# A gated attention, a dense and a routed expert layer in one kernel: routing steps with stated waits, own tiles for one expert's second weights, one ring of four PSUM banks, 512-token dense layers 2 and 3

## Chip, cores and metric

One core of a Trainium2 chip. The metric is the device time of one execution in microseconds, the median of three runs. One execution is also profiled; its rows are read below.

## What is computed

```python
def _attn_ref(q, k, v, alpha):                     # 2 x 8 heads, 768 steps, 48 wide
    for t in range(S):
        state = alpha[:, :, t, :, None] * state + np.einsum('bhd,bhe->bhde', k[:, :, t], v[:, :, t])
        y[:, :, t] = np.einsum('bhd,bhde->bhe', q[:, :, t], state)

def _moe_ref(x, domain_probs, w1, w2):             # 1536 tokens x 384, 4 experts, 1024 hidden
    p = domain_probs / (domain_probs.sum(-1, keepdims=True) + 1e-09)
    for e in range(E):
        out += p[:, e:e + 1] * (np.maximum(x @ w1[e], 0.0) @ w2[e])

def _moe2_ref(x, w_gate, w_noise, noise, w1, w2):  # 8 experts, the best two of each token
    noisy = x @ w_gate + np.log1p(np.exp(x @ w_noise)) * noise
    top2 = np.argpartition(-noisy, 2, axis=1)[:, :2]
    top2_w = softmax of the two noisy logits
    out[token] += top2_w[token, k] * (np.maximum(x[token] @ w1[e], 0.0) @ w2[e])
```

The attention's output, with the heads side by side, is the x of the dense layer, whose output is the x of the routed one.

## The kernel before

Everything is one program on one core, its order written out by hand: generators emit instructions step by step, and each engine works through its own in that order. The work goes through these stages.

The attention runs in groups of 128-token blocks, woven into dense expert 0. Dense experts 1 and 2 (`for e in range(1, E1 - 1)`, line 952) run alone, in units of 384 tokens. Dense expert 3 runs in `main` (line 970), with the routing of the layer behind it as the `side` generator (line 958). Then come eight routed experts on gathered rows, in falling order of their load. The fullest is taken as expert `E1` + 0 (called expert 4 here, the next expert 5), whatever its number.

A matrix product in full precision is made of three: each operand is split into a high half (rounded to fp32r) and the rest, and low x high, high x low and high x high are added up in PSUM. `Weights` loads a quarter of one weight matrix at a time into one of four `raw` tiles (on SP's DMA queue), ACT copies out the high half (line 137), and GpSimd (to expert 4) or DVE (after it) subtracts for the low half (line 138). `W.step`, called at each main step, emits one such preparation as soon as the tiles that it overwrites have been used (`self.done`).

One unit of an expert is 8 calls of `hidden` (line 446; 9 matmuls into one PSUM bank, `hh` by ACT at line 461, `hl` by DVE at line 462, which frees the bank) and then, per block of 128 tokens, 24 matmuls of `product` (line 466) into one bank, read by DVE into `acc` (line 499). Each call of `hidden`, and each 6 matmuls of `product`, is a main step. `hidden` takes its banks from a ring of two (`g1`), `product` from another ring of two (`g2`). Two more banks are `tr`, one each `sc0` and `sc1`.

`drive` (line 506) runs main steps and lets 1.3 steps of `side` follow each. A bare `yield` in `side` is one such step. `route(g)` takes three 128-token blocks: when their rows are done, TensorE turns them (`turned_rows`), makes the gate's logits, and `choose` (line 623) goes on: `uu`, `sp` by ACT; `dl`, `nl`, the maxima and their indices, `sel` and `mask` by DVE; rank matmuls (lines 666 to 672); `spos`, `pos`, `row`, `ge`, `Aoh`, `wt`, `B4`, `VB`, `BV` by DVE; 12 matmuls (line 716) that add these rows to the lists of each expert in `sc0`. After three of four groups, `all_but_last` makes the row numbers `ig_a` of the first two slots of expert 4, gathers their rows (`xg`, an indirect DMA issued on GpSimd), and `side` turns them (`turn`, line 857; `xth` by ACT, `xtl` by DVE). Expert 4 starts on these 256 rows (`moe2(0, 0, 2)`) while the last group is routed. `the_last` then does the same with `ig_b` for the other two slots, ranks the experts by load (`places`), starts the loads of expert 5's weights, whose number SP reads from `places`, and makes the lists of all others (`ig_c`). The other two slots are turned, and `moe2` goes on.

## Time and profile before

| what | us |
|---|---|
| median of 3 runs | 787.21 |
| lowest of 3 runs | 786.96 |
| the profiled execution, its own time | 787.36 |
| its span, first to last instruction | 785.6 |
| TensorE busy in it | 760.1 |
| DVE busy | 351.6 |
| ACT busy | 250.1 |
| GpSimd busy | 170.1 |

The span is what the rows speak of; 1.76 us of the profiled execution lie around it. The ends of matmuls are modelled and overlap the next one's start, so the cost of a matmul is read from start to start, and a busy share of TensorE near 100% doesn't say that it computes at its peak.

### The profile page before, as it was taken

What the parts mean: (1) busy time and instruction counts of PE and PEld (TensorE: products, weight loads), DVE (VectorE), ACT (ScalarE), POOL (GpSimd) and SP (SyncE); (2) the same over time, 40 slices, a digit from 0 to 9 for tenths busy, and PEclk for the clock granted to TensorE, in tenths of its full rate; (3) what the DMA queues carried; (4) which work ended last, traced back from release to release, by engine and by line L of the source; (5) the groups of instructions that cost most, each with busy time, mean ns of one, the idle gap of its engine ahead of it and who ended that gap; (6) DMA issues with size and microseconds to landing.
All of it is one profiled execution on the core that took longest, in us unless ns stands there. A gap on an engine that the chain in (4) does not pass through costs nothing.

```text
span 785.6 us, 12222 instructions
## 1 busy us (share of the span) xinstructions
PE 760.1 (97%) x4774; PEld 734.3 (93%) x4774; DVE 351.6 (45%) x856; ACT 250.1 (32%) x497; POOL 170.1 (22%) x177
## 2 busy tenths in 40 slices
PE   7999999999999999999999999989899999999994
PEld 5889999999999999999999999988799999999994
DVE  5677665763222222222222425445664554554540
ACT  2433222232411223111122313424344444444330
POOL 2410000000510013100041000143342424423331
PEclk7799999999999999999999999999999999999998
DMA  9844412100630003100032000120664655655510
GB/s 169 188 112 88 85 31 41 22 1 1 191 91 1 1 20 101 41 1 1 20 89 67 18 31 10 58 85 11 215 190 131 195 165 153 193 179 164 161 61 30
DMA packets 97998, 66.97 MB, mean 85 GB/s; under 512 B 57577, under 2 KB 94500, under 8 KB 97936
## 3 DMA queue, kind: packets, MB, share of 16 engines
q1 hardware_dynamic: 89008, 51.92, 25.0%
q0 software_dynamic: 5024, 14.13, 5.7%
q8 instruction: 39, 0.64, 0.4%
q10 hardware_dynamic: 3904, 0.10, 0.4%
q14 instruction: 23, 0.19, 0.1%
HBM read 56.69 MB, written 9.82 MB: 85 GB/s over the span
## 4 chain that ended last, share of the span: by engine, by line
PE 68%; issue 14%; POOL 7%; DVE 4%; DMA 4%; ACT 1%; POOLq 0%; DVEq 0%; ACTq 0%
PE g L470 9%; PE g L472 9%; PE g L471 9%; PE g L456 9%; PE g L457 9%; PE g L458 9%; POOL pv L853 2%; PE tr L279 2%; PE sc L371 2%; POOL xg L853 2%; DMA out_dram<-yo,si_c 2%; PE sc L331 2%; POOL out_dram L883 2%; PE sc L345 1%; PE sc L367 1%
## 5 line engine op out<-in xcount | busy, mean ns | idle before, releaser
L461 ACT ACTIVATE hh<-g 128x384 fp32r<-128x384 f32 (+7 forms) x216 | 99.4, 461 | 288.1 <-PE g L458 283.6
L462 DVE SCALAR_TENSOR_TENSOR hl<-g,hh 128x384 fp32r<-128x384 f32 (+7 forms) x216 | 112.3, 521 | 168.6 <-ACT hh L461 168.4
L470 PE MATMUL g<-w2h,hl 128*128 128x384 f32 x464 | 161.0, 347 | 0.0
L472 PE MATMUL g<-w2h,hh 128*128 128x384 f32 x464 | 156.9, 338 | 0.0
L471 PE MATMUL g<-w2l,hh 128*128 128x384 f32 x464 | 156.7, 338 | 0.0
L456 PE MATMUL g<-xh,w1l 128*128 128x384 f32 (+1 forms) x408 | 134.9, 331 | 1.0 <-DVE hl L462 1.0
L457 PE MATMUL g<-xl,w1h 128*128 128x384 f32 (+1 forms) x408 | 131.7, 323 | 0.0
L458 PE MATMUL g<-xh,w1h 128*128 128x384 f32 (+1 forms) x408 | 131.5, 322 | 0.0
L138 POOL TENSOR_TENSOR w1l<-raw,w1h 128x768 fp32r<-128x768 f32 x20 | 37.4, 1876 | 323.2 <-ACT w1h L137 191.3
L471 PEld LDWEIGHTS g<-w2l,hh 128*128 128x128 f32 x464 | 87.5, 189 | 0.0
L470 PEld LDWEIGHTS g<-w2h,hl 128*128 128x128 f32 x464 | 87.3, 188 | 0.2
L472 PEld LDWEIGHTS g<-w2h,hh 128*128 128x128 f32 x464 | 87.2, 188 | 0.0
L456 PEld LDWEIGHTS g<-xh,w1l 128*128 128x128 f32 x408 | 76.7, 188 | 2.2 <-DVE hl L462 2.2
L457 PEld LDWEIGHTS g<-xl,w1h 128*128 128x128 f32 x408 | 76.8, 188 | 0.3 <-DVE xl L396 0.3
L458 PEld LDWEIGHTS g<-xh,w1h 128*128 128x128 f32 x408 | 76.7, 188 | 0.0
L456 PE MATMUL g<-xth,w1l 128*128 128x256 f32 (+6 forms) x216 | 73.9, 342 | 2.6 <-DVE hl L462 1.5
L499 DVE SCALAR_TENSOR_TENSOR acc<-g,prob,acc 128x384 f32<-128x384 f32 x36 | 22.2, 617 | 118.8 <-PE g L472 118.8
L457 PE MATMUL g<-xtl,w1h 128*128 128x256 f32 (+6 forms) x216 | 71.3, 330 | 0.2 <-DVE xtl L868 0.2
L458 PE MATMUL g<-xth,w1h 128*128 128x256 f32 (+6 forms) x216 | 71.3, 330 | 0.0
L137 ACT ACTIVATE w2h<-raw 128x768 fp32r<-128x768 f32 x44 | 37.2, 845 | 29.1 <-issue 16.1
L883 POOL DMA_INDIRECT out_dram<-yo,si_c x26 | 27.0, 1039 | 86.9 <-DVE yo L882 83.8
L456 PEld LDWEIGHTS g<-xth,w1l 128*128 128x128 f32 x216 | 40.7, 188 | 4.0 <-issue 1.6
(182 smaller groups left out, 1070.6 us busy)
## 6 DMA issues: line engine op xcount, KB each, us to landing
raw<-in_moe_w_dram SPq DMA_DIRECT2D x92, 384.0 KB, 3.3
v<-in_v_dram SPq DMA_DIRECT2D x12, 192.0 KB, 3.8
out_dram<-zero SPq DMA_DIRECT2D x1, 2304.0 KB, 11.1
x2d<-acc SPq DMA_DIRECT2D x12, 192.0 KB, 1.9
x_a<-in_alpha_dram SPq DMA_DIRECT2D x20, 96.0 KB, 3.0
x_k<-in_k_dram SPq DMA_DIRECT2D x18, 96.0 KB, 3.1
x_q<-in_q_dram SPq DMA_DIRECT2D x18, 96.0 KB, 3.2
acc<-in_moe_w_dram SPq DMA_DIRECT2D x4, 384.0 KB, 5.6
```

The lines of the kernel that those rows point to most:

```text
L137: nc.scalar.activation(hi, r, AF.Copy)
L138: (nc.gpsimd if e <= E1 else nc.vector).tensor_sub(lo, r, hi.bitcast(F32))
L456: nc.tensor.matmul(t[:, :n], wl, hx[:, kd, t0:t0 + n], start=(kd == 0), stop=False)
L457: nc.tensor.matmul(t[:, :n], wh, lx[:, kd, t0:t0 + n], start=False, stop=False)
L458: nc.tensor.matmul(t[:, :n], wh, hx[:, kd, t0:t0 + n], start=False, stop=(kd == KD - 1))
L461: nc.scalar.activation(hh[:, :n], t[:, :n], AF.Relu)
L462: nc.vector.scalar_tensor_tensor(hl[:, :n], t[:, :n], 0.0, hh.bitcast(F32)[:, :n], op0=OP.max, op1=OP.subtract)
L470: nc.tensor.matmul(t[:m, :DM], hl[:, o:o + m], wh, start=(f == 0), stop=False)
L471: nc.tensor.matmul(t[:m, :DM], hh[:, o:o + m], wl, start=False, stop=False)
L472: nc.tensor.matmul(t[:m, :DM], hh[:, o:o + m], wh, start=False, stop=(f == KF - 1))
L853: nc.gpsimd.indirect_dma_start(out=t[:n, :], out_offset=None, in_=out if prev else x2d[:upto, :], in_offset=bass.IndirectOffsetOnAxis(ap=S ...
L883: nc.gpsimd.indirect_dma_start(out=parts_of_out[s], out_offset=bass.IndirectOffsetOnAxis(ap=SLOT[e * SB + s][2][:n, e * SB + s:e * SB + s ...
```

## The change

The order of preparation takes expert 4's second weights before its first, into a pool of their own (`ownpool`, open from dense expert 3 on), subtracted on GpSimd; its first weights are subtracted on DVE. Expert 5's second weights wait for dense expert 3's only. All first- and second-layer outputs share one ring of four banks (`g`; where `ps("g2", 2)` stood, `ps("g", 4)` stands). Dense experts 1 and 2 take units of 512 tokens, their hidden tiles in a pool `hpool`, whose place `ownpool` takes after them. In `drive`, what `side` yields is the number of main steps until its next step. `choose` works in bursts with stated waits. The first gathered slots are turned in step with the last group's routing (`together`). The loads of expert 5's weights are emitted after the gather of its rows, and SP reads from a copy of `places`.

```diff
@@ Weights
-            self.order = [(e, t, g) for e in range(E1 + E2) for t in ((1, 2) if e else (2, 1))
+            self.order = [(e, t, g) for e in range(E1 + E2) for t in ((2, 1) if e in (0, E1) else (1, 2))
                           for g in range(NG)]
...
-            hi = wpool.tile([P, KD * FG * P], F32R, tag=f"w{t}h", name=f"w{t}h", bufs=NG)
-            lo = wpool.tile([P, KD * FG * P], F32R, tag=f"w{t}l", name=f"w{t}l", bufs=NG)
+            own = (e, t) == (E1, 2)
+            pool = self.own if own else wpool
+            hi = pool.tile([P, KD * FG * P], F32R, tag=f"w{t}h", name=f"w{t}h", bufs=NG)
+            lo = pool.tile([P, KD * FG * P], F32R, tag=f"w{t}l", name=f"w{t}l", bufs=NG)
             nc.scalar.activation(hi, r, AF.Copy)
-            (nc.gpsimd if e <= E1 else nc.vector).tensor_sub(lo, r, hi.bitcast(F32))
+            (nc.gpsimd if e < E1 or own else nc.vector).tensor_sub(lo, r, hi.bitcast(F32))
...
-                if e == 0 or (e - 1, t, g) in self.done:
+                if (e, t) == (E1, 2):
+                    free = self.own is not None
+                elif t == 2 and e == E1 + 1:
+                    free = (e - 2, t, g) in self.done
+                else:
+                    free = e == 0 or (e - 1, t, g) in self.done
+                if free:
                     self.prep()
@@ hidden
+    hidden_in = [(wpool, CAP)]
     def hidden(e, f, hx, lx, t0, n, H_):
-        t = ps("g1", 2)
+        t = ps("g", 4)
...
-        hh = wpool.tile([P, CAP], F32R, tag=f"hh{f}", name="hh")
-        hl = wpool.tile([P, CAP], F32R, tag=f"hl{f}", name="hl")
+        pool, cap = hidden_in[-1]
+        hh = pool.tile([P, cap], F32R, tag=f"hh{f}", name="hh")
+        hl = pool.tile([P, cap], F32R, tag=f"hl{f}", name="hl")
@@ drive
         due = 0.0
+        pace = n_main / n_side if n_side else float("inf")
+        wait = pace
...
-            due += n_side / n_main
-            while side is not None and due >= 1:
-                due -= 1
+            due += 1
+            while side is not None and due >= wait:
+                due -= wait
                 try:
-                    next(side)
+                    said = next(side)
+                    wait = pace if said is None else said
@@ before dense expert 1
+    hst = ExitStack()
+    hidden_in.append((hst.enter_context(tc.tile_pool(name="hpool", bufs=1, side="right")), 4 * P))
@@ choose
         V_.tensor_mul(dl, dl, w)
-        yield
+        yield 2
...
         V_.tensor_add(nl, tl[:, :, :E2], nl)
-        yield
...
             V_.max_index(mi[:, i, :], mx[:, i, :], nl[:, i, :])
-        yield
...
         nc.scalar.activation(ex, ex, AF.Exp)
-        yield
-        yield
+        yield 2
...
         nc.tensor.matmul(o, ones_b, sofar[:, None, :].to_broadcast(b3), start=False, stop=True)
-        yield
...
             V_.tensor_reduce(pos, spos.rearrange("x c b e -> x (c b) e"), axis=AX.X, op=OP.add)
-        yield
...
                          row[:, :, None].to_broadcast([P, 2 * UB, P]), op=OP.is_equal)
+        yield 1
...
         V_.tensor_mul(wt[:, 1, :], ex, wt[:, 0, :])
-        yield
-        if not last:
-            yield
...
                              VB[:, j, :, None, :].to_broadcast(b5), op=OP.mult)
-        yield
-        yield
-        yield
-        yield
+        yield 3
@@ route
+        for i in range(BL):
             while b0 + i not in rows_done:
-                yield
-            yield
...
+                yield 0.5
+            yield 1
+            turned_rows(g, i, b0 + i)
+            yield 1
+            logits(g, i)
         yield from choose(g, b0, BL)
@@ the_last
-        W.ranked = places
-        while W.n_raw - W.n_prep < 4:
-            W.load()
...
         gather(1, 0, blocks(1))
+        nc.vector.tensor_copy(ordered, places)
+        W.ranked = ordered
+        while W.n_raw - W.n_prep < 4:
+            W.load()
@@ dense experts 1 and 2, and side
-        for t0 in range(0, N, 3 * P):
-            drive(moe1(e, t0, 3 * P), bg=W.step)
+        for t0 in range(0, N, 4 * P):
+            drive(moe1(e, t0, 4 * P), bg=W.step)
+    hidden_in.pop()
+    hst.close()
+    own = ExitStack()
+    W.own = own.enter_context(tc.tile_pool(name="ownpool", bufs=1, side="right"))
...
+    def together(*gens):
+        now = 0.0
+        due = [(0.0, i, g) for i, g in enumerate(gens)]
+        while due:
+            due.sort(key=lambda z: z[:2])
+            t, i, g = due.pop(0)
+            if t > now:
+                yield t - now
+                now = t
+            said = next(g, "done")
+            if said != "done":
+                due.append((now + said, i, g))
...
         yield from all_but_last()
-        yield
-        for i in range(2):
-            yield
-            turn(0, i)
-        turned.append(True)
-        yield from route(NB // BL - 1)
+        def first_rows():
+            for i in range(2):
+                yield 6 - 4 * i
+                turn(0, i)
+            turned.append(True)
+        yield from together(first_rows(), route(NB // BL - 1))
         yield from the_last()
```

## Rows read from the trace of the kernel before

**Rows 1.** The page's first part: busy us (share of the span) x instructions.
```profile
PE 760.1 (97%) x4774; PEld 734.3 (93%) x4774; DVE 351.6 (45%) x856; ACT 250.1 (32%) x497; POOL 170.1 (22%) x177
```

**Rows 2.** Stretches: us, then busy us (x instructions) by engine, granted clock, DMA share, GB/s.
```profile
core 0: us, PE busy (x) PEld busy (x) DVE busy (x) ACT busy (x) POOL busy (x), PEclk, DMA share, GB/s
...
200.00:500.00 300.00, 300.00 (x1760) 298.97 (x1759) 82.24 (x193) 71.22 (x133) 43.36 (x47) 1.00 0.15 45
500.00:560.00 60.00, 51.81 (x345) 48.54 (x344) 33.62 (x118) 21.56 (x42) 26.67 (x24) 1.00 0.27 84
560.00:774.00 214.00, 213.33 (x1240) 208.12 (x1239) 113.61 (x172) 93.22 (x160) 76.83 (x75) 1.00 0.50 155
```

**Rows 3.** Waits of TensorE: who waited for whom, us in total, times, longest.
```profile
PE g L456 <- DVE hl L462: 2.5, 4, 1.0
PE tr L865 <- DMA xg<-x2d,ig_b: 1.8, 1, 1.8
PE sc L716 <- DVE BV L706: 1.5, 1, 1.5
PE tr L865 <- DMA xg<-x2d,ig_a: 1.4, 1, 1.4
...
PE g L456 <- ACT xth L867: 0.6, 1, 0.6
...
PE g L456 <- DVE sp L643: 0.5, 1, 0.5
```

**Rows 4.** Timeline of TensorE: start us, us, instruction (384, 256 and 432 columns).
```profile
258.25 0.34 PE L456 MATMUL g<-xh,w1l 128*128 128x384 f32 x1
...
270.74 0.34 PE L470 MATMUL g<-w2h,hl 128*128 128x384 f32 x1
...
531.11 0.28 PE L456 MATMUL g<-xth,w1l 128*128 128x256 f32 x1
...
532.76 0.29 PE L458 MATMUL g<-xth,w1h 128*128 128x256 f32 x1
...
576.75 0.36 PE L456 MATMUL g<-xth,w1l 128*128 128x432 f32 x1
...
590.50 0.36 PE L458 MATMUL g<-xth,w1h 128*128 128x432 f32 x1
```

**Rows 5.** Timeline of DVE in the hand-over: groups 2 and 3 of the choice.
```profile
506.46 1.72 DVE L659 TENSOR_TENSOR mask<-sel 128x24 bf16<-128x24 f32 x1
...
537.35 0.17 DVE L643 TENSOR_TENSOR sp<-sp,dl 128x24 f32<-128x24 f32 x1
...
539.73 0.18 DVE L659 TENSOR_TENSOR mask<-sel 128x24 bf16<-128x24 f32 x1
...
543.20 0.19 DVE L675 TENSOR_TENSOR spos<-sel,tr 128x48 f32<-128x48 f32 x1
...
543.87 0.96 DVE L686 TENSOR_TENSOR Aoh<-iota_i,row 128x768 f32<-128x768 int32 x1
...
546.01 0.63 DVE L706 TENSOR_TENSOR BV<-sel,VB 128x192 f32<-128x192 f32 x2
...
553.13 0.19 DVE L736 SCALAR_TENSOR_TENSOR si_c<-LR,emp 128x32 int32<-128x32 f32 x1
```

**Rows 6.** Groups of DVE by shape: count, busy us, mean ns, idle before and releaser.
```profile
L462 DVE SCALAR_TENSOR_TENSOR hl<-g,hh 128x384 fp32r<-128x384 f32 x120 | 66.7, 556 | 116.7 <-ACT hh L461 116.7
...
L138 DVE TENSOR_TENSOR w1l<-raw,w1h 128x768 fp32r<-128x768 f32 x28 | 26.8, 958 | 4.8 <-ACT w1h L137 3.4 <-PE g L458 0.3
```

**Rows 7.** Timeline of GpSimd in the hand-over: one low-half subtraction.
```profile
506.27 1.87 POOL L138 TENSOR_TENSOR w1l<-raw,w1h 128x768 fp32r<-128x768 f32 x1 [3.58 <-ACT w1h L137]
```

**Rows 8.** The chain that ended last: start us, us, what.
```profile
521.03 3.22 DMA xg<-x2d,ig_a
...
546.70 1.57 PE sc L716 x12
...
550.27 5.44 DMA xg<-x2d,ig_b
```

**Rows 9.** Timeline of SP's queue: the loads of expert 5's first weights.
```profile
551.36 2.42 SPq L116 DMA_DIRECT2D raw<-in_moe_w_dram  x4
```

More of the change, by code (lines that the diff above doesn't have):

```diff
@@ L504, in moe1, with drive @@
             yield
-    def drive(main, side=None, n_main=1, n_side=0, bg=None, finish=True):
+    def drive(main, side=None, n_main=1, n_side=1, bg=None, finish=True):
         due = 0.0
+        pace = n_main / n_side if n_side else float("inf")
+        wait = pace
         for _ in main:
@@ L591 @@
     places = const.tile([P, E2], U32, name="places")
+    ordered = const.tile([P, E2], U32, name="ordered")
     gates = const.tile([P, NB, E2], F32, name="gates")
@@ L650, in choose @@
             V_.max(mx[:, i, :], nl[:, i, :])
-        ex = small("ex", [UB])
         for i in range(UB):
             V_.max_index(mi[:, i, :], mx[:, i, :], nl[:, i, :])
-        yield
         sel = small("sel", [2, UB, E2])
@@ L659, in choose @@
         V_.tensor_add(mask, sel[:, 0], sel[:, 1])
+        ex = small("ex", [UB])
         V_.tensor_sub(ex, mx[:, :, 1], mx[:, :, 0])
         nc.scalar.activation(ex, ex, AF.Exp)
-        yield
-        yield
+        yield 2
         tp = ps("tr", 2)
@@ L740, in route @@
         b0 = g * BL
-        def there(i):
+        for i in range(BL):
             while b0 + i not in rows_done:
-                yield
-            yield
-        yield from there(0)
-        turned_rows(g, 0, b0)
-        yield
-        yield from there(1)
-        turned_rows(g, 1, b0 + 1)
-        yield
-        logits(g, 0)
-        yield
-        yield from there(2)
-        yield
-        turned_rows(g, 2, b0 + 2)
-        logits(g, 1)
-        if b0 + BL < NB:
-            yield
-            yield
-        logits(g, 2)
+                yield 0.5
[3 more added lines that the diff above has]
+            logits(g, i)
         yield from choose(g, b0, BL)
@@ L773, in all_but_last @@
         while not mp:
-            yield
+            yield 0.5
         gather(0, 0, 2, upto=N - BL * P)
@@ L777, in all_but_last @@
         nc.tensor.matmul(tn[:, :1], ones_b, sofar[:, 0:1], start=True, stop=True)
-        yield
         free = small("free", [1])
@@ L781, in all_but_last @@
         nc.vector.tensor_scalar(shift[:1, :, 0], free[:1].to_broadcast([1, BL]), 0.0, None, op0=OP.max)
-        yield
     def ranks(name, shape, dt=F32):
@@ L794, in the_last @@
         gather(0, 2, SB)
-        yield
+        yield 1
         tn = ps("tr", 2)
@@ L798, in the_last @@
         nc.tensor.matmul(tn[:, :E2], ones_b, shift[:, 0, :], start=False, stop=True)
-        yield
         key = ranks("key", [E2])
@@ L919, in moe2 @@
         for d in range(KD):
-            t = ps("g2", 2)
+            t = ps("g", 4)
             for f in range(KF):
@@ L987 @@
     mp["st"].close()
+    own.close()
     rst.close()
```

13 lines of the change are left out of this document (6 added, 7 removed).

## The prediction

> **What bounds the kernel now.** The page's first part, read first, has TensorE busy for 97% of the span and no other engine above 45% [rows 1]. An average hides stages, so the stretches come next [rows 2]. From 200 to 500 us TensorE has no idle time that the modelled ends show; from 560 to 774 us it has 0.67 us; what follows 774 us is the last rows' scatter. From 500 to 560 us it is busy for 51.81 of 60 us: this hand-over (last dense unit, choice of experts, first gathered rows) holds 8.2 us, and nearly all else is matmul work. The clock is at its upper level (1.00) in all three. The waits view names the idle time [rows 3]: an eviction (hl, line 462) that frees a PSUM bank, the lists' input BV, two gathers, and small ones. So two things can move the time: what TensorE's work costs, and these waits. Start (0 to 200 us) and tail keep their order of work and are taken as unchanged.
>
> **512 tokens in dense layers 2 and 3.** Where nothing interrupts, 72 matmuls of 384 columns go from 258.25 to 270.74 us, 12.49 us, 173.4 ns each. 14 steps of 256 columns take 1.65 us, 117.9 ns; 71 steps of 432 columns take 13.75 us, 193.7 ns [rows 4]. These are start to start; the 338 ns of one matmul in the groups contains overlap. The slope is 0.434 ns a column below 384 and 0.423 above it, so 512 columns are estimated at 227.5 to 229.0 ns. One expert has 288 first-layer matmuls now (49.94 us) and 216 after (49.14 to 49.46 us): 0.5 to 0.8 us less, 1.0 to 1.6 us for two; I take 1.4, by the nearer width. The second layer keeps its 128x384 form. Evictions become a third longer and a quarter fewer, under 72 / 8 x 0.228 = 2.05 us of matmuls each: covered.
> The Trainium skill ("TensorE: Matmul & The Clock Gate", "Wait — 56ns, not 53.3ns?") gives a warm matmul a fixed 2.5 ns over its columns at 2.4 GHz. Removing 144 matmuls would then save 0.36 us, and the sum below would be 782.4. The trace's 173.4 ns at 384 columns stand 13.4 ns over 160 ns, so the row speaks for the larger saving here; that page's figure was taken in bf16.
>
> **The ring of four PSUM banks.** Now two banks serve first-layer outputs and two serve second-layer ones, so the third first-layer tile waits until the first has been read. That is the largest wait, 2.5 us in four events [rows 3], two of them in the hand-over, where DVE was held in the choice. In one ring of four a tile waits for the fourth before it: three tiles of slack (4.7 us at 384 tokens, 3.2 at 256) against a delay of about 1 us. I take all 2.5 us away; bounds 1.5 and 3 us, the latter with the restart. What is late next is the choice itself, costed below. No other user of these banks holds one for long: a second-layer tile is read 0.6 us after its last matmul.
>
> **Choice in one burst, stated waits.** A bare yield was 1/1.3 of a main step; a number now means main steps. Counting both orders by hand gives for each group of three blocks: logits, two steps, DVE burst to `mask`, two steps, rank matmuls and the next burst, one step, weights and BV, three steps, lists. (A main step is nine first-layer matmuls, 1.56 us at 384 columns and 1.06 at 256, or six second-layer ones, 1.05 us.)
> Price on DVE, from the last group where nothing disturbed it [rows 5]: sp to mask 537.35 to 539.91, 2.56 us, less 0.4 for an eviction between: 2.15. spos through Aoh 543.20 to 544.83, 1.6. From there through BV, to 546.64, less 0.3 for an eviction, 1.5. An eviction of 384 columns takes DVE 0.556 us [rows 6], one of 256 about 0.4.
> Mask to rank: two steps give 3.1 us (384) or 2.1 us (256); needed are the eviction of the tile before, about 1.0 to 1.2 us, and 2.15. That is a wait of 0.2 us in three groups and 0.9 in the last. Rank to lists: two hidden and two product steps give 5.2 us, or 4.2 in the last group. DVE needs two held evictions (1.1 or 0.8), 1.6, one more eviction (0.55 or 0.4), 1.5: 4.8, or 4.3. So no wait in groups 0 and 1 and about 0.4 in the last with the signals. In group 2, DVE also gets the low halves of expert 4's first weights, which GpSimd made before, at 0.96 us each [rows 6]; two fall in this stretch: 4.8 + 1.9 - 5.2, about 1.3 with one of them partly in a gap. Queued behind them are evictions, which the ring now forgives, and BV, which it does not. Against that stands a gain already counted in: before, GpSimd's 1.87 us subtraction starts at 506.27 and DVE's mask beside it takes 1.72 us, against 0.18 in the last group [rows 5, 7]; sm and one more small operation are stretched alike. With these subtractions off GpSimd that goes.
> Waits after: 0.6 + 0.9 + 1.3 + 0.4 = 3.2 us. The ones they replace are BV 1.5 and sp 0.5 [rows 3]. Net +1.2 us. Bounds: 2.0 us gained if the bursts always come in time, 2 us lost more if ACT's table loads (not shown above) hold the evictions or both weight subtractions fall before BV.
>
> **The gathers.** The first gather (two slots) now makes TensorE wait 1.4 us. It follows the lists of group 2, and the first transpose is now stated six product steps (6.3 us) after it, 7.9 us after those lists begin (12 matmuls, 1.57 us). GpSimd's second issue came 3.6 us after the lists began where nothing else held it (546.70 to 550.27), and a transfer beside no other takes 3.2 us [rows 8]: 6.8 us together. Gone: -1.4 us (bound 0). The second gather is now waited for 1.8 us. From the lists' start to its landing: 546.70 to 555.71, 9.0 us, of which 5.44 in transfer against 3.22 for the first [rows 8]. Four weight loads are issued at 551.36, into this transfer [rows 9]. After, those loads wait for `ordered`, copied behind the ranking and the third lists. Line 736's last result is there at 553.32 [rows 5], so the loads come at least 2 us later than now, and the transfer should be like the first: 6.8 us. Six product steps and the lists give 7.9 us of matmul work from the same point. Gone: -1.8; if the transfer stays at 5.44, about 0.8 of it. The transpose and eviction between the last slot and its first matmul (0.6 us [rows 3]) have nothing beside them in either order: 0.
>
> **Own tiles for expert 4's second weights.** Loads, ACT copies and GpSimd subtractions move from the hand-over to the first unit of dense layer 4. There no choice runs, and over the stretch from 200 to 500 us ACT is busy for 71 of 300 us and GpSimd for 43 [rows 2]; SP's queue no longer has four loads ahead of the row stores. TensorE waited for none of these, so the gain is 0 beyond what is counted. Expert 5's second weights may now be prepared before expert 4's are used up; as a copy is queued when its load is issued, not landed, ACT can be held behind a transfer, and transposes behind ACT. Bounds: 0, and +2 us if one lands late; before, TensorE shows no wait of that kind after 560 us [rows 2, 3], so 0. The later load of expert 5's first weights is inside the same bound.
>
> **Sum.** 787.36 us (profiled execution; 785.6 span and 1.76 outside it; the median 787.21 is 0.15 lower) - 1.4 - 2.5 + 1.2 - 1.4 - 1.8 = 781.4 us. A difference of about 2% (16 us) is what a measurement of this kernel can tell from no change.
>
> **Rivals.** *The waits only move*: DVE's extra work eats what the ring gives and the second gather stays slow: +3 instead of +1.2, and 0.8 for 1.8, and a late load's 1 to 2: 785 to 787. For it: DVE ends the wait in most rows of [rows 3], and it gets more work. Against: the ring takes evictions off TensorE's path. *All closes*: no wait is left but the one for the last eviction: 787.4 - 1.6 - 3 - 2 - 1.4 - 1.8, about 777.5; with the small gaps around each restart 776. For it: the matmuls have enough steps in nearly every place counted. Against: group 2's sum. *Wide matmuls do not scale* (slower): in dense layers 2 and 3, 432 matmuls of 512 columns replace 576 of 384 that take 99.9 us. If one takes over 243 ns, 105 us in all, the whole other gain of 4.5 us and more is eaten; at 250 ns the time is 787.4 - 4.5 + 8.1 = 791. Against it: the slope falls between 384 and 432 columns [rows 4]. *The order does not come out as stated* (a step's fraction carries a burst past its place): one more main step in two places, 1 us each, 783.5; inside the forecast.
>
> **How the numbers follow.** Forecast case (779 to 784.5) 0.58; waits move (to 787) 0.21; all closes (to 776) 0.14; slower by wide matmuls or by something unnamed 0.05; lower than 776, 0.02. No case that the rows allow reaches 2% faster: hand-over 8.2, later evictions 0.7 and 1.6 make 10.5 us. So faster 0.02, same 0.95, slower 0.03. The range, 776.0 to 787.0, takes both neighbours in.
>
> **What would show it.** Hidden matmuls of 512 columns at 227 to 229 ns from start to start in a stretch that begins where it did before; no wait on hl; none on the first gather; a second gather of about 3.2 us with the loads issued after it lands; waits on mask and BV in the last two groups, the larger in group 2, with a low-half subtraction ahead of BV on DVE; small DVE operations at 0.2 us throughout. The prediction falls if dense layers 2 and 3 don't shorten by 1 to 1.6 us, if ACT stands behind a weight load after the hand-over, or if the choice costs TensorE over 5 us.

## The result, and the profile after

The changed kernel takes 778.17 us (median of four runs, 777.92 to 778.69) against 787.09 us for the kernel before in the same comparison: a ratio of 0.9891, interval 0.9871 to 0.991. That is 1.1% faster, and the interval excludes 1, but by the 2% bound it counts as no difference. The prediction said 781.4 us, 776.0 to 787.0, and no difference by 2%. One of the four runs of the kernel before took 2456.77 us; the median counts it, the ratio leaves it out. The profiled execution takes 778.11 us with a span of 776.4 us, 9.2 us less than the span before.

The page's first part:

```profile
PE 756.7 (97%) x4630; PEld 714.2 (92%) x4630; DVE 347.9 (45%) x845; ACT 246.5 (32%) x481; POOL 161.8 (21%) x173
```

The busy shares by engine answer to [rows 1] and have hardly moved; again it is the stretches that say something. The table of stretches after (us, then busy us by engine, granted clock, DMA share, GB/s):

```profile
200.00:500.00 300.00, 300.00 (x1619) 279.80 (x1619) 80.11 (x178) 71.48 (x120) 50.72 (x51) 1.00 0.16 50
500.00:560.00 60.00, 57.10 (x403) 55.15 (x402) 37.63 (x133) 23.54 (x49) 11.52 (x16) 1.00 0.26 82
560.00:764.00 204.00, 204.00 (x1171) 199.45 (x1170) 107.66 (x162) 87.06 (x149) 76.05 (x75) 1.00 0.50 156
```

Against [rows 2], the hand-over has 2.9 us of idle TensorE instead of 8.2, and the 0.67 us behind it are gone. GpSimd's share of the hand-over fell from 26.67 to 11.52 us: weight subtractions that it made there are made elsewhere. The waits of TensorE in that stretch (who waited for whom, us in total, times, longest), to be held against [rows 3]:

```profile
PE sc L729 <- DVE BV L722: 1.1, 2, 0.9
PE tr L686 <- DVE mask L679: 0.8, 1, 0.8
PE g L470 <- ACT xth L865: 0.6, 1, 0.6
PE g L471 <- DVE xtl L866: 0.3, 1, 0.3
```

No row for hl and none for a gather is left. What remains is the choice (BV, mask) and the split of the last gathered slot (xth, xtl). TensorE's timeline (start, duration, instruction, in brackets the idle time before it and its releaser):

```profile
274.44 0.39 PE L470 MATMUL g<-xh,w1l 128*128 128x512 f32 x1
...
291.24 0.34 PE L485 MATMUL g<-w2h,hl 128*128 128x384 f32 x1
...
512.20 1.55 PE L729 MATMUL sc<-BV,Aoh 128*128 128x64 f32 x12 [0.89 <-DVE BV L722]
...
535.28 0.19 PE L686 MATMUL tr<-mask,upper 128*128 128x24 bf16 x1 [0.77 <-DVE mask L679]
...
540.12 1.55 PE L729 MATMUL sc<-BV,Aoh 128*128 128x64 f32 x12 [0.24 <-DVE BV L722]
...
548.02 0.82 PE L863 MATMUL tr<-ident,xg 128*128 128x128 f32 x6
```

From 274.44 to 291.24 us there are 72 matmuls of 512 columns: 16.80 us, 233.3 ns each, not 227.5 to 229. The waits in brackets are in group 2 of the choice (BV 0.89, none on mask) and in the last group (mask 0.77, BV 0.24). At 548.02 the second gather's two slots are turned without a wait. DVE beside it:

```profile
505.47 0.18 DVE L679 TENSOR_TENSOR mask<-sel 128x24 bf16<-128x24 f32 x1
...
507.12 0.96 DVE L142 TENSOR_TENSOR w1l<-raw,w1h 128x768 fp32r<-128x768 f32 x1 [0.18 <-ACT w1h L141]
...
511.44 0.70 DVE L722 TENSOR_TENSOR BV<-sel,VB 128x192 f32<-128x192 f32 x2
...
546.17 0.17 DVE L816 COPY ordered<-places 128x8 uint32<-128x8 uint32 x1
```

Group 2's `mask` takes 0.18 us where it took 1.72 [rows 5]. One low-half subtraction (507.12) stands between the burst to `mask` and the one to BV. The order is copied at 546.17; SP's queue issues the loads behind it (SP's timeline):

```profile
547.11 2.29 SPq L118 DMA_DIRECT2D raw<-in_moe_w_dram  x4
```

They were issued at 551.36 before, into the gather [rows 9], 1.1 us after its second transfer; now they follow that transfer's issue by 3.4 us, though on the clock they come 4.2 us earlier. The DMA view of the second transfer alone, issued at 543.70 after and at 550.27 before (issuer, kind, count, us from issue to landing), after and then before:

```profile
xg<-x2d,ig_b POOLq DMA_INDIRECT x1, 3.7
```

```profile
xg<-x2d,ig_b POOLq DMA_INDIRECT x1, 5.4
```

After, it lands at 547.42: 7.3 us after the lists began (540.12), 0.3 us after the loads were issued and 0.6 us before the turn at 548.02.

Stage by stage, from the first matmul of each stage in the two timelines of TensorE:

| stage | before, us | after, us | difference |
|---|---|---|---|
| up to dense expert 1 | 207.99 | 207.54 | -0.45 |
| dense experts 1 and 2 (layers 2 and 3, the 512-token units) | 200.91 | 200.71 | -0.20 |
| dense expert 3, with choice groups 0 to 2 | 121.77 | 118.93 | -2.84 |
| expert 4, slots 0 and 1, with the last group | 26.28 | 22.29 | -3.99 |
| expert 4, slots 2 and 3 | 19.80 | 18.78 | -1.02 |
| rest | 208.85 | 208.15 | -0.70 |

So 7.9 of the 9.2 us come from the three stages from dense expert 3 to the end of expert 4, which hold the hand-over, and the wider units give next to nothing. Which edit earns that, the trace alone can't say: the experiments undo them one at a time.

### The profile page after: what moved, and what is told of

The parts are those of the page before. It is cut to its first block, busy times and chain, and to the rows that moved or that the text cites. A ratio compares the mean times of both kernels' runs of the same rounds, so it can differ in the third digit from the quotient of the medians.

```text
span 776.4 us, 11869 instructions
## 1 busy us (share of the span) xinstructions
PE 756.7 (97%) x4630; PEld 714.2 (92%) x4630; DVE 347.9 (45%) x845; ACT 246.5 (32%) x481; POOL 161.8 (21%) x173
## 4 chain that ended last, share of the span: by engine, by line
PE 94%; DVE 3%; ACT 1%; issue 0%; POOL 0%; POOLq 0%; DVEq 0%; ACTq 0%
PE g L470 13%; PE g L471 13%; PE g L472 13%; PE g L485 10%; PE g L487 10%; PE g L486 10%; PE g L922 3%; PE g L924 3%; PE g L923 3%; PE sc L382 3%; PE tr L290 3%; PE sc L342 2%; PE sc L356 1%; PE tr L863 1%; PE sc L378 1%; PE sc L641 1%
## 5 line engine op out<-in xcount | busy, mean ns | idle before, releaser
L476 ACT ACTIVATE hh<-g 128x384 fp32r<-128x384 f32 (+8 forms) x200 | 96.6, 485 | 278.6 <-PE g L472 274.2
L477 DVE SCALAR_TENSOR_TENSOR hl<-g,hh 128x384 fp32r<-128x384 f32 (+8 forms) x200 | 109.7, 550 | 162.9 <-ACT hh L476 160.5
L470 PE MATMUL g<-xh,w1l 128*128 128x512 f32 (+2 forms) x360 | 126.8, 352 | 0.0
L471 PE MATMUL g<-xl,w1h 128*128 128x512 f32 (+2 forms) x360 | 124.3, 345 | 0.0
L472 PE MATMUL g<-xh,w1h 128*128 128x512 f32 (+2 forms) x360 | 124.2, 345 | 0.0
L142 POOL TENSOR_TENSOR w1l<-raw,w1h 128x768 fp32r<-128x768 f32 x16 | 29.3, 1837 | 281.7 <-ACT w1h L141 281.7
L471 PEld LDWEIGHTS g<-xl,w1h 128*128 128x128 f32 x360 | 67.9, 189 | 6.5 <-DVE xl L407 0.3
L472 PEld LDWEIGHTS g<-xh,w1h 128*128 128x128 f32 x360 | 67.7, 188 | 6.4
L470 PEld LDWEIGHTS g<-xh,w1l 128*128 128x128 f32 x360 | 67.8, 188 | 6.2
L922 PE MATMUL g<-hh,w2l 128*128 128x432 f32 (+4 forms) x120 | 43.4, 362 | 0.0
```

What stands on the lines that cost most here:

```text
L142: (nc.gpsimd if e < E1 or own else nc.vector).tensor_sub(lo, r, hi.bitcast(F32))
L470: nc.tensor.matmul(t[:, :n], wl, hx[:, kd, t0:t0 + n], start=(kd == 0), stop=False)
L471: nc.tensor.matmul(t[:, :n], wh, lx[:, kd, t0:t0 + n], start=False, stop=False)
L472: nc.tensor.matmul(t[:, :n], wh, hx[:, kd, t0:t0 + n], start=False, stop=(kd == KD - 1))
L476: nc.scalar.activation(hh[:, :n], t[:, :n], AF.Relu)
L477: nc.vector.scalar_tensor_tensor(hl[:, :n], t[:, :n], 0.0, hh.bitcast(F32)[:, :n], op0=OP.max, op1=OP.subtract)
```

## The experiments

Times are medians, against 778.17 us for the changed kernel and 786.5, 786.5 and 787.5 us for the kernel before in the three groups of runs. The changed kernel itself was not timed again beside them, so differences below 1 us between groups decide nothing by themselves; where they matter the stages of the traces are read.

Two things in the profiles must be kept apart from the edits. The first is the start: from 29.4 to 29.9 us the granted clock is 0.50 in the profiles of before, after, e3, e6 and e7 and 1.00 in the other nine, and up to dense expert 1 the five take 207.3 to 208.1 us, the nine 205.9 to 206.9. So a total can differ by 1 us with nothing done. The second is the clock in the hand-over, which fell to its lower level for some microseconds in the profiles of e3, e6, e7, e10, e11 and e12 and in none of the others. The three hand-over stages of the table above together (us):

| kernel | hand-over stages, us | clock fell in them |
|---|---|---|
| before | 167.85 | no |
| after | 160.00 | no |
| e1_two_rings | 163.69 | no |
| e2_384 | 160.07 | no |
| e3_384_wide_tiles | 161.53 | yes |
| e5_tiles_528 | 159.78 | no |
| e6_loads_early | 163.13 | yes |
| e7_lo_gpsimd | 162.60 | yes |
| e8_old_steps | 160.46 | no |
| e9_steps_mended | 159.55 | no |
| e10_before_late_loads | 171.28 | yes |
| e11_before_ring | 166.58 | yes, twice |
| e12_no_own_tiles | 164.46 | yes |

(e4_widths, which leaves work out, stands apart.) Edits are to the changed kernel unless said otherwise.

**Two rings again (e1_two_rings).**

```diff
-        t = ps("g", 4)
+        t = ps("g1", 2)
...
-            t = ps("g", 4)
+            t = ps("g2", 2)
```

> The changed kernel with its two rings of two banks back (first-layer outputs g1, second-layer outputs g2), all else as changed. Theory R (the ring is worth more than the named waits on hl, because at 256 columns each first-layer tile also waits a little for a bank): slower than the changed kernel by 2.5 to 4.5 us, with waits on hl in the hand-over, and the last unit of dense expert 1 again at 9.2 us for 72 matmuls instead of 8.4. Rival (the stated waits already keep DVE out of the way, so two banks would do): slower by less than 1 us, no wait on hl over 0.3 us.

781.08 us (780.94 to 782.34), ratio 0.9941, 0.9928 to 0.9955: 2.9 us slower than the changed kernel. The waits view, first row:

```profile
PE g L470 <- DVE hl L477: 4.4, 7, 1.0
```

The bank wait is back, with seven events where [rows 3] had four; the hand-over stages take 3.7 us longer. The last 256-column hidden stage of dense expert 0 (72 matmuls, long before any choice; the expectation counts this expert as 1) takes 9.24 us again, as before (9.23), against 8.44 after. It is 9.23 or 9.24 in all three kernels with two rings (before, e1, e10) and 8.42 to 8.74 in those with one: up to 0.8 us in a place where the waits view names nothing, presumably by bank waits too short to be listed.

**Units of 384 tokens again (e2_384).**

```diff
-        for t0 in range(0, N, 4 * P):
-            drive(moe1(e, t0, 4 * P), bg=W.step)
+        for t0 in range(0, N, 3 * P):
+            drive(moe1(e, t0, 3 * P), bg=W.step)
```

(The hidden tiles also go back to the pool where they stood before.)

> The changed kernel with dense layers 2 and 3 in units of 384 tokens again, hidden tiles of 432 columns in the old pool. Theory W (512 columns cost 233 ns, more than a straight line from 256, 384 and 432 columns): the first-layer matmuls at 173.4 ns give back 0.85 us, and the time changes by less than 0.5 us either way. Rival, the prediction's line: 1.0 to 1.6 us slower than the changed kernel.

778.2 us (777.44 to 778.79), ratio 0.9902, 0.9887 to 0.9917: nothing lost. TensorE's timeline, one unit:

```profile
206.43 0.34 PE L470 MATMUL g<-xh,w1l 128*128 128x384 f32 x1
...
218.91 0.34 PE L485 MATMUL g<-w2h,hl 128*128 128x384 f32 x1
...
231.53 0.34 PE L470 MATMUL g<-xh,w1l 128*128 128x384 f32 x1
```

72 first-layer matmuls take 12.48 us (173.3 ns) and 72 second-layer ones 12.62 us (175.3 ns); the two experts last 200.8 us. In the changed kernel the second layer is at 173.5 ns (96 matmuls in 16.66 us). That gives its balance: first layer 432 x 233.2 for 576 x 173.4, +0.9 us; second layer 576 x (173.5 - 175.3), -1.0 us. The wider unit itself loses 0.9 us, and a side effect on the second layer pays it back.

**384 tokens, hidden tiles as in the change (e3_384_wide_tiles).** The loop of e2_384 alone; the tiles stay in the new pool with their 512 columns.

> The same 384-token units, but hidden tiles of 512 columns in the new pool, of which 384 are used. It asks why second-layer matmuls in dense layers 2 and 3 fell from 175.0 to 173.4 ns. Theory A (where the tiles lie, 2048 instead of 1728 bytes apart): 173.4 ns here, and with 384-column first-layer matmuls at 173.4 ns the two layers take 199.8 us, 0.9 less than as changed. Rival (the blocks follow each other differently in units of four): 175.0 ns here too, and the two layers take 200.9 us.

777.54 us (777.29 to 780.66), ratio 0.989, 0.9875 to 0.9905. Its trace has the second layer at 12.49 us a unit (173.5 ns), so that side effect belongs to where or how large the hidden tiles lie and not to the 512 tokens. But the first layer goes to 12.71 us (176.5 ns) from its second unit on, and the two experts together to 201.4 us. Half the theory held: the second layer, which reads the hidden tiles, goes with them. What moves the first layer, which doesn't read them and whose first unit still takes 173.4 ns, isn't shown.

The profiled run is the one of 780.66 us, 3 us above the other three (777.29 to 777.63). Its choice is that of the changed kernel, and so is its wait on BV in group 2; but behind it the clock is at its lower level (TensorE's timeline and a stretch of e3, then the same stretch of the changed kernel):

```profile
513.23 1.55 PE L729 MATMUL sc<-BV,Aoh 128*128 128x64 f32 x12 [0.89 <-DVE BV L722]
```

```profile
516.00:518.00 2.00, 2.00 (x8) 2.00 (x8) 0.66 (x1) 0.00 (x0) 1.58 (x1) 0.50 0.00 0
```

```profile
516.00:518.00 2.00, 2.00 (x15) 1.97 (x14) 0.62 (x1) 0.36 (x1) 1.64 (x2) 1.00 0.31 67
```

That second-layer stage takes 19.68 us instead of 18.15. So one fall costs 1.5 us here, and the same wait can come with it or without: the profile of one run of a kernel can hold a fall that the edit did not make.

**One width for each unit (e4_widths).** Each of the six units of dense experts 1 and 2 computes another number of first-layer columns; GpSimd sets the rest of its hidden columns to zero. Width and unit so change together, but in the changed kernel all six units are at 233.3 ns.

```diff
+    WD = {(1, 0): 512, (1, 512): 504, (1, 1024): 496, (2, 0): 480, (2, 512): 464, (2, 1024): 448}
...
+        full, n = n, WD.get((e, t0), n)
```

> The changed kernel with the first layer of dense layers 2 and 3 cut to 512, 504, 496, 480, 464 and 448 columns in their six units (the other columns of the hidden tiles are set to zero, so those tokens lose what these layers give). From start to start by unit. Theory W1 (only the full bank of 512 columns is dear): 504 at 224 to 226 ns on the line through 384 and 432, 512 at 233. Theory W2 (the cost over 2.4 GHz grows with width): a smooth bend, 448 at 201 to 203, 480 at 216 to 218, 504 at 229. Rival W3 (the dense stage, not the width, costs 5 ns a matmul, for instance by transfers beside it): every width lies 4 to 6 ns over the line, 448 at 205.

One run, 771.4 us with that work left out. TensorE's timeline around the unit of 448 columns:

```profile
370.01 0.36 PE L472 MATMUL g<-xh,w1l 128*128 128x448 f32 x1
...
384.57 0.34 PE L490 MATMUL g<-w2h,hl 128*128 128x384 f32 x1
```

14.56 us for 72, 202.2 ns. All six, read in the same way, beside a straight line through 384 and 432 columns of [rows 4]:

| columns | ns from start to start | line | over it |
|---|---|---|---|
| 448 | 202.2 | 200.5 | 1.7 |
| 464 | 213.1 | 207.3 | 5.8 |
| 480 | 216.0 | 214.0 | 2.0 |
| 496 | 226.5 | 220.8 | 5.7 |
| 504 | 228.8 | 224.2 | 4.6 |
| 512 | 233.3 | 227.5 | 5.8 |

None of the three expected shapes fits: neither a step at one width nor a steady rise. Theory W2's own three values come out (448, 480 and 504 columns), but 464 and 496 stand off its smooth bend. The excess is real (5.8 ns x 432 = 2.5 us in the change), its cause is open.

**Hidden tiles 16 columns wider (e5_tiles_528).**

```diff
-    hidden_in.append((hst.enter_context(tc.tile_pool(name="hpool", bufs=1, side="right")), 4 * P))
+    hidden_in.append((hst.enter_context(tc.tile_pool(name="hpool", bufs=1, side="right")), 4 * P + 16))
```

> The changed kernel with hidden tiles of 528 columns (2112 bytes apart) of which 512 are used. It asks whether the pitch of a 512-column matmul hangs on where the tiles lie. Theory A (it does: at 384 columns the same code ran at 173.5 and at 176.5 ns in two placements): first-layer matmuls of dense layers 2 and 3 leave 233.2 ns by over 2 ns, and second-layer ones leave 173.5. Rival (the width sets it): 233.2 ns to within 0.5, and no change in time.

One run, 778.62 us. The first layer stays at 16.79 us a unit (233.2 ns): its excess isn't made by the tile that the results go to. The second layer goes from 16.66 to 16.97 us (173.5 to 176.8 ns): it reads those tiles, and their place does move it.

**The four loads before the gather (e6_loads_early).**

```diff
+        W.ranked = places
+        while W.n_raw - W.n_prep < 4:
+            W.load()
...
         gather(1, 0, blocks(1))
-        nc.vector.tensor_copy(ordered, places)
-        W.ranked = ordered
-        while W.n_raw - W.n_prep < 4:
-            W.load()
```

> The changed kernel with the loads of expert 5's weights started where they were before, right after the ranking and ahead of its gather, from the places themselves. Theory L (the second gather was slow because these loads ran into it): its second transfer takes 5 us or more instead of 3.9, TensorE waits 1 to 2 us on it again, and the time is 0.8 to 2 us longer. Rival (the choice reached its lists earlier, that was all): the transfer stays under 4.3 us, no wait on it, time within 0.4 us.

781.8 us (779.77 to 781.9), ratio 0.9934, 0.992 to 0.9947: 3.6 us slower. The waits view and the chain that ended last:

```profile
PE tr L861 <- DMA xg<-x2d,ig_b: 1.5, 1, 1.5
```

```profile
544.27 6.16 DMA xg<-x2d,ig_b
```

The transfer takes 6.16 us beside the loads, and TensorE waits 1.5 us for it: the mechanism of the prediction, at its size. The rest of the 3.6 us is in the stretches behind that wait:

```profile
548.00:553.00 5.00, 2.72 (x18) 2.04 (x17) 1.73 (x3) 0.98 (x2) 3.42 (x5) 1.00 0.99 326
553.00:555.00 2.00, 2.00 (x12) 2.00 (x12) 0.42 (x1) 0.38 (x1) 1.57 (x2) 0.52 0.89 310
```

TensorE is busy for 2.72 of the first 5 us; then the granted clock is 0.52 for two us, and 1.00 again from 557 us. 256-column matmuls come every 0.21 us there, 0.12 otherwise, and that stage takes 10.94 us instead of 9.43: 1.5 us. The hand-over stages take 3.1 us longer in all, 1.6 by the wait and 1.5 by the clock. One of the five timed runs was at 779.77, with a mean granted clock of 0.983 against 0.981 to 0.982 in the other four; it may be one without the fall, but only one run was profiled.

**All of expert 4's subtractions on GpSimd (e7_lo_gpsimd).**

```diff
-            (nc.gpsimd if e < E1 or own else nc.vector).tensor_sub(lo, r, hi.bitcast(F32))
+            (nc.gpsimd if e <= E1 else nc.vector).tensor_sub(lo, r, hi.bitcast(F32))
```

> The changed kernel with the low halves of expert 4's first weights subtracted on GpSimd again. Theory G (GpSimd's subtraction and DVE's small operations hold each other up): mask, sm or wt of group 2 take 1 us or more where one overlaps, which costs DVE about what the four subtractions of 0.96 us cost it now, so the wait on BV of group 2 stays between 0.5 and 1.5 us and the time within 0.7 us. Rival (DVE's own subtractions make that wait): it goes, and the time falls by 0.7 to 1 us.

779.84 us (779.57 to 780.79), ratio 0.9919, 0.9905 to 0.9933: 1.7 us slower. Waits, then DVE's timeline, then GpSimd's:

```profile
PE sc L729 <- DVE BV L722: 2.4, 2, 2.1
```

```profile
510.55 1.62 DVE L712 TENSOR_TENSOR wt<-ex,wt 128x3 f32<-128x3 f32 x1
```

```profile
510.34 1.82 POOL L142 TENSOR_TENSOR w1l<-raw,w1h 128x768 fp32r<-128x768 f32 x1 [1.60 <-ACT w1h L141]
```

An operation on three columns ends when GpSimd's subtraction ends: 1.62 us where it takes 0.16. It stands on the way to BV, whose wait in group 2 grows from 0.89 to 2.1 us. Behind that wait the clock fell here too (stretch):

```profile
516.00:518.00 2.00, 2.00 (x7) 2.00 (x7) 0.00 (x0) 0.00 (x0) 1.53 (x2) 0.50 0.00 0
```

The hand-over stages take 2.6 us longer, 1.2 by the wait and the rest with the clock. Moving these subtractions to DVE (0.96 us each) costs DVE time and takes 1.2 us off TensorE's wait. The mechanism is as theory G had it; the size is above what it gave by the fall, which in e3_384_wide_tiles came without this cause.

**The old steps (e8_old_steps).** `choose`, `route`, `all_but_last`, `the_last` and `side` as before, with 1.3 steps for each main step; all else as changed.

```diff
-        yield 2
+        yield
...
-        yield from together(first_rows(), route(NB // BL - 1))
+        yield
+        for i in range(2):
+            yield
+            turn(0, i)
+        turned.append(True)
+        yield from route(NB // BL - 1)
```

> The changed kernel with the old steps: route, choose, the first slots' turning and the last group one after the other, a bare yield as 1/1.3 of a main step. The ring, the own tiles, the 512-token units and the late loads stay. Theory S (the stated steps are worth the gathers' waits, less what the new waits on mask and BV cost): 2 to 3.5 us slower, with a wait on the first gather of over 1 us. Rival (the ring does nearly all; the old steps under four banks are as good): within 1 us.

777.52 us (776.66 to 778.44), ratio 0.9888, 0.9873 to 0.9903: not slower than with the stated steps. Its waits in the hand-over:

```profile
PE tr L890 <- DMA xg<-x2d,ig_a: 1.3, 1, 1.3
...
PE tr L689 <- DVE mask L682: 0.5, 1, 0.5
...
PE tr L890 <- DMA xg<-x2d,ig_b: 0.2, 1, 0.2
```

The first gather's wait is back, and BV's are gone. Stated steps trade one for the other; the sum of named waits in the hand-over, 2.8 us, is the same in both kernels. The second gather stays almost free without the stated order, since the loads come late in this kernel too.

**Three steps moved (e9_steps_mended).**

```diff
-        yield 2
+        yield 3 if last else 2
...
-        yield 3
+        yield 3 if last else 4
...
+        yield 3
+        turn(0, 2)
...
-    for i in range(2, SB):
-        turn(0, i)
+    turn(0, 3)
```

The first stated wait is the one from `mask` to the rank matmuls, the second the one from BV to the lists.

> The changed kernel with three places moved by one step each: the lists of groups 0 to 2 one main step later (for the wait of 0.9 us on BV), the last group's rank matmuls one step later (for 0.8 us on mask), and slot 2 of expert 4 turned one product step ahead of slot 3. Theory M (these waits are order, not work): 1.2 to 2 us faster than the changed kernel, the first wait gone, of the last group's two at most 0.5 left. Rival (they move on into the second gather, whose landing leaves only about 0.6 us): a wait of 0.5 us or more on it, and under 1 us faster.

776.96 us (776.13 to 777.03), ratio 0.9863, 0.9848 to 0.9878: the lowest time of all that do the whole work, 1.2 us below the changed kernel. In the hand-over stages the difference is only 0.45 us; 0.8 lies in the start, which the edit doesn't touch, so the 1.2 to 2 us expected are not shown. Its waits in the hand-over:

```profile
PE tr L776 <- DVE sofar L734: 0.9, 1, 0.9
...
PE sc L729 <- DVE BV L722: 0.5, 1, 0.5
```

The wait on mask and group 2's 0.89 us wait on BV are gone, but one of 0.9 us on `sofar` takes the latter's place: DVE brings this count up to date behind the lists, and the matmul that reads it now follows the lists with too little matmul work between.

**Late loads alone, in the kernel before (e10_before_late_loads).** The edit of e6_loads_early reversed, on the kernel before.

> The kernel before with one part alone: the loads of expert 5's weights start behind its gather and the third lists, from a copy of the places. Theory L: the second transfer falls from 5.4 to about 3.9 us, the wait on it from 1.8 to 0.5 us or less, 1 to 2 us faster than before. Rival (without the earlier lists the gather lands too late anyway): under 0.7 us.

788.94 us (787.72 to 790.03, 11 runs in two groups, 787.7 to 788.0 and 788.9 to 790.0), ratio 1.0015, 1.0005 to 1.0025: no gain, a miss. Waits, then a stretch:

```profile
PE g L456 <- issue: 2.0, 1, 2.0
...
PE tr L866 <- DMA xg<-x2d,ig_b: 0.2, 1, 0.2
```

```profile
558.00:560.00 2.00, 1.29 (x7) 0.99 (x5) 0.22 (x1) 0.64 (x3) 0.06 (x1) 0.50 0.89 318
```

The wait for the gather fell from 1.8 to 0.2 us, and the first hidden tile behind it starts at 555.57 instead of 556.95, 1.1 us of which lie in the start (206.85 us instead of 207.99). It had still waited 2.0 us for the split of the last slot, whose releaser the profile doesn't show ("issue"): ACT begins that split at 555.03, 1.4 us after the turn's last matmul. Then the clock is at its lower level (0.50) and the stage of 72 matmuls takes 14.12 us instead of 10.43. What one wait gave, the stretch behind it took back, and more: the hand-over stages take 3.4 us longer than before in this profile, of which the start and the stretch behind expert 4 give back 1.8. Why ACT was late with that split stays open.

**The ring alone, in the kernel before (e11_before_ring).** The edit of e1_two_rings reversed, on the kernel before.

> The kernel before with one part alone: one ring of four banks for both layers' outputs. Theory R: no wait on hl is left, 72 matmuls of 256 columns in the last unit of dense expert 1 take 8.4 us instead of 9.2, but where the hand-over is held by the second gather the waits it frees are lost again: 1.5 to 3 us faster. Rival (all of the ring's worth shows alone): 3 us or more.

782.99 us (782.31 to 783.16), ratio 0.994, 0.9927 to 0.9954: 4.5 us faster than the kernel before, half of the whole gain. Its waits have no row for hl. The second gather's 1.8 us of [rows 3] stands; the wait on BV has grown to 2.2, one of 0.9 on mask is new, and the first gather's 1.4 and the 0.5 on sp are gone:

```profile
PE sc L716 <- DVE BV L706: 2.2, 2, 1.5
PE tr L865 <- DMA xg<-x2d,ig_b: 1.8, 1, 1.8
```

and behind the second of them the clock fell (stretch):

```profile
554.00:556.00 2.00, 2.00 (x11) 2.00 (x11) 0.42 (x1) 0.38 (x1) 1.02 (x1) 0.50 1.07 364
```

It fell once more, from 516 to 520 us (0.57 to 0.58). So in this profile only 1.3 of the 4.5 us lie in the hand-over stages; the rest is 0.8 us in the 256-column unit of e1_two_rings, 0.7 us behind expert 4, and the start. By the time the rival holds (3 us or more), and without the falls the ring alone would presumably have given more; the hand-over stages alone don't decide between the two.

**No own tiles (e12_no_own_tiles).** Expert 4's weights are prepared in the old order and into the shared tiles; its second ones are still subtracted on GpSimd, its first ones on DVE.

```diff
-            self.order = [(e, t, g) for e in range(E1 + E2) for t in ((2, 1) if e in (0, E1) else (1, 2))
+            self.order = [(e, t, g) for e in range(E1 + E2) for t in ((1, 2) if e else (2, 1))
...
-            pool = self.own if own else wpool
+            pool = wpool
...
-                if (e, t) == (E1, 2):
-                    free = self.own is not None
...
+                free = e == 0 or (e - 1, t, g) in self.done
```

> The changed kernel without own tiles: expert 4's second weights are prepared after its first ones, in the hand-over, into the tiles of dense expert 4, with the low halves on GpSimd as before; the first weights' low halves stay on DVE. The prediction's step (TensorE waited for none of this): within 0.7 us. Rival (in the hand-over GpSimd's subtractions stretch DVE's small operations of the last group, as they did those of group 2): 1 to 2.5 us slower, with an operation of 1 us or more among them.

782.64 us (781.21 to 783.28), ratio 0.9938, 0.9925 to 0.9952: 4.5 us slower than the changed kernel. Waits, then two stretches around them, then DVE's and GpSimd's timelines:

```profile
PE tr L680 <- DVE mask L673: 2.5, 1, 2.5
```

```profile
534.00:536.00 2.00, 0.40 (x7) 0.40 (x8) 1.36 (x13) 0.35 (x2) 0.00 (x0) 1.00 0.00 0
536.00:540.00 4.00, 4.00 (x22) 4.00 (x21) 3.77 (x8) 1.91 (x5) 1.83 (x1) 0.57 0.00 0
```

```profile
532.46 1.30 DVE L660 TENSOR_TENSOR sp<-sp,dl 128x24 f32<-128x24 f32 x1
...
537.30 1.77 DVE L693 TENSOR_SCALAR row<-pos 128x6 int32<-128x6 int32 x1
```

```profile
531.89 1.83 POOL L142 TENSOR_TENSOR w2l<-raw,w2h 128x768 fp32r<-128x768 f32 x1 [5.55 <-ACT w2h L141]
...
537.21 1.83 POOL L142 TENSOR_TENSOR w2l<-raw,w2h 128x768 fp32r<-128x768 f32 x1 [3.49 <-ACT w2h L141]
```

Without the own tiles these subtractions fall into the last group of the choice, and two small DVE operations (0.17 us each when alone) last until GpSimd is done. TensorE waits 2.5 us for `mask` instead of 0.8, the clock behind that wait is 0.57 for four us, and the stage of 72 matmuls takes 13.47 us instead of 10.45; the next one takes 10.59 instead of 9.43. Of the 1.7 us more on `mask`, the stretch of `sp` is 1.1; about 0.6 comes ahead of `sp`, where ACT's copy of a second weight (530.98, 0.83 us) stands before an eviction. About 1.3 of the 3.0 us of the first stage go with the clock. The edit brings the loads, ACT's copies and GpSimd's subtractions back together; the subtractions alone were not moved.

## Why the prediction was right, and where it was not

The direction, the class and the range held, and so did the place: the hand-over. The middle was 3.2 us too high, by terms that failed in both directions.

**512 tokens: -1.4 predicted, -0.2 measured, 0 when undone.** The step that failed is the extrapolation of the slope from 384 and 432 columns to 512: 233.2 ns against 227.5 to 229.0. The prediction named this as a sign against itself: it falls if dense layers 2 and 3 don't shorten by 1 to 1.6 us. The rival "wide matmuls do not scale" was thus right in kind, and far from its 243 ns. The price per matmul that the Trainium skill gives ("TensorE: Matmul & The Clock Gate", "Wait — 56ns, not 53.3ns?"), by which the saving would be 0.36 us, came nearer in the sum, though not for its reason: at 512 columns the row stands 20 ns over columns at 2.4 GHz (213.3 ns), not 2.5. Nor did the prediction see that the second layer would change pitch with its tiles' place.

**The ring: -2.5 predicted; -2.9 when it alone is undone, -4.5 when it alone is done.** Mechanism right, term too small. It was priced by named waits. What it also removes is short: up to 0.8 us of one 256-column unit long before the hand-over (where "start" was taken as unchanged). In the hand-over stages undoing it costs 3.7 us, where 2.5 were predicted: the changed kernel with two rings waits 4.4 us on hl, the kernel before 2.5. Doing it alone gives 1.3 us there, in a profile with two falls of the clock. That its worth depends on the kernel around it, because DVE in the choice delays the evictions, is likely but not shown.

**Choice and first gather: +1.2 and -1.4 predicted, -0.2 together; undoing the steps gives -0.65, no difference.** The sum is right. The parts were sized less well: no group waits for ranks except the last (0.77; 0.9 predicted), BV waits 0.89 in group 2 (1.3 predicted) and 0.24 in the last (0.4): 1.9 us for 3.2. What was mis-sized: 0.2 us in each of groups 0 to 2, and a second subtraction ahead of BV, which didn't come. The 0.2 us came of a price taken "where nothing disturbed it": `sel` there stood beside a subtraction of GpSimd (537.79 to 539.64) and took 0.53 us (DVE's timeline of the kernel before), where it takes 0.21 after, and sp to mask takes 1.95 us after, not 2.15.

```profile
539.16 0.53 DVE L656 TENSOR_TENSOR sel<-iota_u,mi 128x48 f32<-128x48 uint32 x1
```
As predicted, the first gather isn't waited for, and one subtraction on DVE stands ahead of BV in group 2.

**Second gather: -1.8 predicted, and no wait left.** With the loads early again the transfer takes 6.16 us and is waited for: the mechanism held. The sizes were near: 7.3 us from the lists to the landing for 6.8, 3.7 us of transfer for 3.2, and the loads are issued just ahead of the landing, not behind it; 7.9 us of matmul work covered it with 0.6 to spare. Yet undoing the edit costs the changed kernel 3.6 us (1.5 of it with the clock), and doing it alone gives the kernel before nothing. A term "the wait, and it is gone" misses both: what it costs also depends on the clock granted behind the wait.

**Own tiles: 0 predicted, 4.5 when undone.** This term was put at nothing by the argument "TensorE waited for none of these", true of the loads and copies; but GpSimd's subtractions stretch DVE's small operations, and for those TensorE does wait. The rows showed it, `mask` at 1.72 us beside a subtraction of 1.87 [rows 5, 7], and I counted it for group 2 alone. How much of the 9 us this is stays open: of the 4.5 us about 1.3 go with a fall of the clock and some with ACT's copies, the own tiles were never put alone into the kernel before, and there GpSimd's subtractions of these weights stretch only `sel` in the last group, by 0.3 us. For the first weights, moved to DVE, theory G's mechanism holds; the 1.7 us of their undoing hold a fall of the clock as well.

**The rivals.** *All closes* (776 to 777.5) was nearest; e9_steps_mended reached it at 776.96, e8_old_steps almost, at 777.52. The prediction's bound of about 2% was coarse for this kernel: the interval of the ratio is 0.4% wide. *The waits only move* was true of the choice alone. *The order does not come out as stated* is not seen.

The sum of what single undoings cost, 2.9 + 3.6 + 1.7 + 4.5 = 12.7, is more than the 9 us that the change gives. They may overlap: the same idle microseconds, and slow matmuls behind them, can be brought back by any of four causes. And in the profiles of three of the four undoings the clock fell, which e3_384_wide_tiles shows happening by itself at 1.5 us. Shares that add up can't be given for this change.

## What to carry to other kernels

Where one engine's small operations release another, look for a long operation of a third engine beside each that lasts longer than its twin, and price a move of that third engine's work by the stretched twins, not by whether anyone waits for it by name. Price a wait by the whole stage in which it lies, since the waits view doesn't list all that a stage loses, and the clock can be low behind an idle stretch. Before an undoing is priced by its trace, read the granted clock of that profile stage by stage: a fall or a slow start may belong to the run and not to the edit. And where several edits work against the same idle time, undoing each tells what is needed and doing each alone tells what is enough.

## What the runs showed of the hardware

DVE and GpSimd: operations of 0.16 to 0.18 us lasted 1.30 to 1.85 us when they met a low-half subtraction of 1.82 to 1.85 us on GpSimd, and ended with it (e7_lo_gpsimd, e12_no_own_tiles). The Trainium skill ("SBUF — State Buffer", "Who interferes with whom") has it that a DVE instruction with two inputs in SBUF, or in a two-port mode, and a GpSimd instruction that reads SBUF exclude each other for a whole instruction; the two rows with two SBUF inputs (1.62 and 1.30 us) agree with that, and the one-input operation on `row` (1.77 us) would need the mode.

The clock: it is 1.00 through the hand-over in the profiles of before, after, e1, e2, e4, e5, e8 and e9. In those of e3, e6, e7, e10, e11 (twice) and e12 it fell towards its lower level (0.50 to 0.58 over two to four us, 0.50 being 1.2 GHz), each time behind idle time of TensorE: a wait of 0.89 us in e3, of 2.1 in e7, of 2.0 in e10, of 1.5 and 1.8 in e11, of 2.5 in e12. But the changed kernel had the same 0.89 us and no fall, and the kernel before had 1.8 us and none, so the length of a wait alone doesn't decide; what does was not settled. A fall cost about 1.3 to 1.5 us in e3, e6 and e7. Since only one run of each kernel is profiled, how often it falls isn't known either.

Pitch of fp32r matmuls at 384 columns: the second layer is at 173.5 ns (after, e3), 175.3 (before, e2) or 176.8 (e5), which goes with the place or size of the hidden tiles that it reads; the first layer is at 173.4 or 176.5 (e3 from its second unit on, and one unit of the changed kernel, at 408.25), and what moves it isn't shown. From 448 to 512 columns there is an excess between 1.7 and 5.8 ns over a straight line, that doesn't rise steadily. None of this was explained.
